# A two-layer Strassen kernel: the last visits' y sums are added on VectorE to loaded totals, and the second layer opens on such totals

## The chip, the core and the metric

One NeuronCore of a Trainium2 chip runs the whole program. The metric is device time in microseconds (us) of one execution; lower is better. Engines are named as the profile names them: PE (TensorE), DVE (VectorE), ACT (ScalarE), POOL (GpSimd) and SP (SyncE, which here only issues DMAs).

## The reference

Decayed causal attention gives 2304 tokens of width 512, and two feed-forward layers (512 to 2048 and back) follow. All is float32.

```python
scores = scale * np.matmul(q, k.transpose(0, 1, 3, 2))
ret = scores * Dmat                       # gamma ** (i - j) for i >= j, else 0
x = np.matmul(ret, v)                     # 4 x 8 heads, 576 x 64, laid out as 2304 x 512
h = x @ w_in                              # layer one
g = h * np.tanh(np.log1p(np.exp(np.minimum(h, 20.0))))   # h > 20 uses h inside tanh
x = g @ w_out
h = np.maximum(x @ moe2_w_in, 0.0)        # layer two
out = h * h @ moe2_w_out
```

## The kernel before, in words

**Visits.** The two layers m = 0, 1 are cut into 4 passes p over the 2048 hidden units, and each pass visits the three token blocks v of 768 tokens. That makes 24 visits u, 0 to 11 in layer one and 12 to 23 in layer two. The order of the blocks turns round from pass to pass, so that visits 9 to 11 have the blocks 2, 1, 0, visits 12 to 14 again 2, 1, 0, visits 18 to 20 have 2, 1, 0 and visits 21 to 23 have 0, 1, 2: visits 20 and 21 share block 0.

**Products.** A visit has two halves (fp 0, 1), each a Strassen-Winograd scheme of seven products P1 to P7 (`chain`, line 849 issues the matmuls). A product reads one of seven x operands, the tiles `ring` (ring_71 to ring_77), each held as a high and a low part, so that three matmuls make one product of float32 accuracy. The results pile up in four PSUM banks `h`, with copies of some of them in `cp`. ACT applies mish or relu, DVE or ACT squares, and differences and cuts into high and low parts (L750, L757) make operands `g` for the way back.

**y sums.** From the fourth visit of a layer on, the way back to width 512 is also seven products, R1, R2, R6, R5, R7, R4, R3 (`block_y`, L1002), into four PSUM banks `py`. The sums of visit u are made during visit u + 1, woven between its products; those of visit 23 come at the end. Each R belongs to one of four blocks of y (`R_TO`: R1 and R2 to 0, R4 to 1, R6 and R3 to 2, R5 and R7 to 3). A sum leaves PSUM by an ACT copy into a staging tile (`staging`: st_more, two tiles e, and t2, t3), where R2 is added on DVE to what R1 left (L1011); then POOL issues an accumulating DMA that adds the staging tile into DRAM: into the scratch `sums_d` (xsum_103 to 114, L1021) in layer one, into the output itself in layer two (L1023), whose runs there are 1 KB long. Six accumulates leave per visit.

**The last visit.** `load_total` (L1033) loads the four blocks of token block 2's sums from `out` into `total` (in part_69) at the start of visit 23; visit 23's own sums are added to them on DVE and stored plainly.

**The turn.** Visit 12 needs x operands of layer two for block 2, which is also visit 9's and whose sums are accumulated during visit 10. `again_x` loads blocks of xsum (seven loads, into the low halves of ring tiles and into t2), makes the four differences on DVE (L408, L409, L410, L417) and cuts each operand (`cut_x`: ACT makes the high part, DVE at L291 the low part). In the other visits `fetch` loads ready operands that were saved to DRAM (`ring<-d`).

**The order.** Every instruction goes into a `Plan` with its engine, a cost and the names (keys) that it reads and writes. `due` gives each a due time, working back from the order of the matmuls; `order` then simulates the engines and puts instructions in the order in which it would start them, the earliest due first among those that are ready. Matmuls stay nearly in the written order (`sequences`); DVE, ACT and SP are free to move. SP issues plain DMAs in that one order, and POOL's queue has the accumulates. `hand_over` passes a region of memory from one set of keys to another, here the half of part_69 that holds weights (`wy`) and then `total`.

```python
        if end:
            to, kt = (lambda: total[b]), [("total", b, i) for i in range(2)]
        else:
            to, kt = held.pop(b) if merged else staging(u)
        ...
            if merged or end:
                fn = lambda dst=dst, src=src: nc.vector.tensor_tensor(dst(), src(), dst(), op=ALU.add)
                dve(fn, n, [("py", o), kt[i]], [kt[i]])
            else:
                act(dst, src, n=n, reads=[("py", o)], writes=[kt[i]])
```

Of the kernel before, what the change touches and what calls it, by code (L numbers as in the profile page):

```python
# [19 lines left out]
DM = H * D  # L20
# [209 lines left out]
def kernel(  # L230
# [58 lines left out]
    def pair(op, out, a, b, n, reads, writes):  # L289
        get = lambda t: t() if callable(t) else t  # L290
        dve(lambda: nc.vector.tensor_tensor(get(out), a, get(b).bitcast(F32), op=op), n, reads, writes)  # L291

# [401 lines left out]
    def staging(u):  # L694
        slots = stage if fast(u) else first_stage
        if fast(u) and (u >= turn_m or 2 * NSB <= u < turn_m - 2):
            slots = slots + [(t.rearrange("p j n -> p (j n)"), [k, k]) for t, k in ((t2, "t2"), (t3, "t3"))]
        if u >= nv - 2:
            slots = slots[1:]
# [218 lines left out]
    def sum_keys(m, v, b):  # L918
        return [("sum", m, v, b, i) for i in range(3)]

    def out_block(v, b):
        r = SB * v + b // 2 * TH
        return out[r : r + TH, b % 2 * 256 : b % 2 * 256 + 256].rearrange("(i p) c -> p i c", p=P)

    def y_group(u, th, f):
# [27 lines left out]
        for i, o in enumerate(yb[0]):  # L953
            y = lambda o=o, n=TH if m == 0 else DM: py[o][:, :n]
            if m:
                t, kt = staging(u)
                r = SB * v + TH * th + P * i
                act(t()[:, :DM], y, n=DM, reads=[("py", o)], writes=kt)
                dma(out[r : r + P], t()[:, :DM], kt, [("sum", m, v, 2 * th + d, i) for d in range(2)], P * 4 * DM)
                continue  # L960
# [10 lines left out]
    def block_y(u, name):  # L971
# [4 lines left out]
        b = R_TO[name]  # L976
        end = u == nv - 1
        merged = name in MERGED and not end
        if end:
            to, kt = (lambda: total[b]), [("total", b, i) for i in range(2)]  # L980
        else:
            to, kt = held.pop(b) if merged else staging(u)
            if name == "R1" and "R2" in MERGED:
                held[b] = to, kt
        parts = (TH, TH) if m == 0 else (DM, DM // 2)
        for i, o in enumerate(two):
# [22 lines left out]
            src = lambda o=o, n=n: py[o][:, :n]  # L1009
            if merged or end:  # L1010
                fn = lambda dst=dst, src=src: nc.vector.tensor_tensor(dst(), src(), dst(), op=ALU.add)  # L1011
                dve(fn, n, [("py", o), kt[i]], [kt[i]])
            else:
                act(dst, src, n=n, reads=[("py", o)], writes=[kt[i]])
            if end and name in ("R2", "R7", "R4", "R3"):
                k = ((0, 2), (2, 3))[i]
                src = total[b][:, 256 * k[0] : 256 * k[1]].rearrange("p (i c) -> p i c", c=256)
                dma(out_block(v, b)[:, k[0] : k[1]], src, [kt[i]], [("out", b, i)], P * 4 * n)
        if not end and b not in held:
            if m == 0:  # L1020
                fn = lambda: nc.gpsimd.dma_start(out=sums_d[v][b], in_=in_two(to()), accum_op=ALU.add)  # L1021
            else:
                fn = lambda: nc.gpsimd.dma_start(  # L1023
                    out=out_block(v, b), in_=to().rearrange("p (i c) -> p i c", c=256), accum_op=ALU.add
                )
            plan.add("SP", 0.1, fn, kt, sum_keys(m, v, b), 2.6)
        late_cut = dict(R6=6, R5=2) if u == turn_m - 1 else dict(R1=6, R2=2)
        if name in late_cut or u != turn_m - 1:
# [3 lines left out]

    def load_total():  # L1033
        hand_over(ks_at[1], [("total", b, i) for b in range(4) for i in range(2)])
        v = visits[-1][2]
        for b in (0, 2, 3, 1):
            dst = total[b].rearrange("p (i c) -> p i c", c=256)
            dma(dst, out_block(v, b), sum_keys(1, v, b), [("total", b, i) for i in range(2)], P * 8 * TH)

# [47 lines left out]
    for u in range(nv + 1):  # L1087
# [15 lines left out]
        if u == turn_m + NSB:  # L1103
            free_ops[:] = [ahead[j] for j in (2, 4, 3, 1, 0)]
            free_raws.sort(key=lambda j: (j + 4) % 8)
            assert len(free_raws) == 8
        if u == nv - 1:
            load_total()
        pos = u % NSB
        for fp, seq in enumerate(sequences(u)):  # L1110
            if u in (NSB, turn_m + NSB):
                for name in ("R5", "R7", "R4", "R3") if fp else ("R1", "R2", "R6"):
                    split_block(name, visits[u][0])
            if (u, fp) == (1, 1):
                hand_over(part_keys(1), ks_at[1])
# [6 lines left out]
            for name in seq:  # L1122
# [121 lines left out]
```

## Time and profile before

| what | value |
|---|---|
| three timed runs | 803.25, 804.91, 805.34 us, median 804.91 |
| the profiled execution | 805.24 us, of which the span in the trace is 803.5 |
| mean granted clock of PE | 0.992 |
| busy: PE, PEld | 98%, 96% |
| busy: DVE, ACT, POOL | 82%, 70%, 15% |
| DMA | 212.07 MB, mean 264 GB/s |
| accumulates from staging, L1021 and L1023 | issued by POOL, 384 KB each |

The trace is of one execution. Busy shares are of its span; PE is the matmul pipe and PEld the weight loads beside it. The granted clock is a share of full speed. The time outside the span, 805.24 - 803.5 = 1.7 us, is start and end.

### The profile page before, as it was taken

To read this page: it belongs to the slowest core of one execution; us is meant where nothing else is said; L and a number is where in the kernel's file an instruction comes from. 1 tells how busy PE (TensorE), PEld (TensorE's weight loads), DVE (VectorE), ACT (ScalarE), POOL (GpSimd) and SP (SyncE) were. 2 spreads that over 40 slices of the span, in tenths; PEclk is the share of its full clock that TensorE was granted. 3 is DMA by queue.
4 is the path that set the end of the run, shared out by engine and by line. 5 is a ranking of instruction groups with operands and counts; after the bars stand their busy time and mean duration, and the time that the engine had idled before them with its cause. 6 is when DMAs were issued, how large, how long until landed. Compare 5 with 4: busy or idle time off the path is not lost.

```text
span 803.5 us, 14615 instructions
## 1 busy us (share of the span) xinstructions
PE 786.3 (98%) x5582; PEld 769.7 (96%) x5582; DVE 655.1 (82%) x1114; ACT 560.2 (70%) x1119; POOL 119.7 (15%) x122
## 2 busy tenths in 40 slices
PE   8999999999999999999989999999999999999797
PEld 7999999999999999998989898999999999999797
DVE  5799998887999875994768768989889977975537
ACT  1697667675887676875767677877788777885552
POOL 3200000001122111111110100001221231321220
PEclk9999999999999999999998999999999999999999
DMA  9984887369998997799999999669988999699975
GB/s 330 405 334 158 321 299 311 116 257 339 326 235 205 325 327 161 146 328 286 261 294 278 306 328 401 237 215 338 330 173 172 339 293 235 108 295 216 278 130 123
DMA packets 72966, 212.07 MB, mean 264 GB/s; under 512 B 6592, under 2 KB 29760, under 8 KB 72896
## 3 DMA queue, kind: packets, MB, share of 16 engines
q1 hardware_dynamic: 45920, 171.02, 56.6%
q0 software_dynamic: 26976, 40.11, 31.1%
q8 instruction: 44, 0.72, 0.4%
q14 instruction: 26, 0.21, 0.1%
HBM read 125.39 MB, written 85.72 MB: 263 GB/s over the span
## 4 chain that ended last, share of the span: by engine, by line
PE 85%; DVE 6%; DMA 6%; ACT 1%; issue 1%; SPq 1%; DVEq 0%; POOLq 0%; ACTq 0%
PE h L849 39%; PE py L1002 30%; PE py L944 12%; DMA ring<-d 2%; PE h L535 2%; PE py L589 1%; DMA out_dram<-t 1%; DMA out_dram<-e 1%; DVE ring L291 1%; DVE a L543 1%; PE py L553 1%; PE py L567 1%; DMA qk<-in_qk_dram 1%; DMA xraw<-part 1%; DVE g L750 1%
## 5 line engine op out<-in xcount | busy, mean ns | idle before, releaser
L849 PE MATMUL h<-ring,win 128*128 128x384 f32 x1932 | 369.3, 337 | 9.0 <-ACT cp L280 4.2
L849 PEld LDWEIGHTS h<-ring,win 128*128 128x128 f32 x1932 | 337.1, 189 | 11.6 <-ACT cp L280 4.4
L750 DVE TENSOR_TENSOR g<-part,g 128x768 fp32r<-128x768 f32 x126 | 119.3, 955 | 47.3 <-ACT g L280 47.0
L1002 PE MATMUL py<-wout,g 128*128 128x256 f32 x1134 | 147.7, 282 | 0.7 <-DVE g L750 0.7
L1002 PEld LDWEIGHTS py<-wout,g 128*128 128x128 f32 x1134 | 144.9, 190 | 0.9 <-DVE g L750 0.9
L1002 PE MATMUL py<-g,wout 128*128 128x384 f32 x756 | 144.5, 335 | 0.0
L1002 PEld LDWEIGHTS py<-g,wout 128*128 128x128 f32 x756 | 133.1, 189 | 0.0
L280 ACT ACTIVATE g<-part 128x768 fp32r<-128x768 f32 x126 | 105.0, 843 | 13.2 <-DVE part L757 8.4
L280 ACT ACTIVATE cp<-h 128x384 f32<-128x384 f32 x138 | 67.5, 489 | 38.9 <-PE h L849 37.9
L280 ACT ACTIVATE part<-h 128x384 f32<-128x384 f32 x108 | 52.7, 488 | 26.2 <-DVE h L832 19.7
L757 DVE TENSOR_TENSOR part<-part 128x768 f32<-128x768 f32 x72 | 66.6, 956 | 4.4 <-ACT part L280 3.0
L280 ACT ACTIVATE part<-py 128x384 f32<-128x384 f32 (+1 forms) x98 | 47.4, 509 | 30.2 <-PE py L944 17.0
L832 DVE TENSOR_TENSOR h<-h,cp 128x384 f32<-128x384 f32 x92 | 51.8, 564 | 16.6 <-PE h L849 16.5
L280 ACT ACTIVATE e<-py 128x384 f32<-128x384 f32 (+1 forms) x88 | 41.4, 489 | 23.8 <-PE py L1002 23.2
L1021 POOL DMA_DIRECT2D xsum<-part x19 | 16.9, 941 | 261.5 <-DVE part L1011 203.0
L1023 POOL DMA_DIRECT2D out_dram<-t x21 | 27.7, 1383 | 178.0 <-DVE t L1011 120.7
L944 PE MATMUL py<-g,wout 128*128 128x384 f32 x288 | 53.5, 335 | 0.4 <-DVE wout L291 0.4
L280 ACT ACTIVATE t<-py 128x512 f32<-128x512 f32 (+2 forms) x60 | 29.1, 489 | 33.5 <-PE py L1002 25.4
L944 PE MATMUL py<-wout,g 128*128 128x512 f32 x216 | 51.2, 391 | 0.0
L944 PEld LDWEIGHTS py<-g,wout 128*128 128x128 f32 x288 | 50.2, 188 | 0.7 <-DVE wout L291 0.7
L944 PEld LDWEIGHTS py<-wout,g 128*128 128x128 f32 x216 | 40.4, 188 | 8.0
L1021 POOL DMA_DIRECT2D xsum<-e x26 | 22.6, 880 | 92.3 <-ACT e L280 72.2
(95 smaller groups left out, 981.7 us busy)
## 6 DMA issues: line engine op xcount, KB each, us to landing
ring<-d SPq DMA_DIRECT2D x77, 768.0 KB, 8.6
raw<-in_wp_dram SPq DMA_DIRECT2D x64, 512.0 KB, 6.3
d<-ring SPq DMA_DIRECT2D x42, 768.0 KB, 7.4
xsum<-e POOLq DMA_DIRECT2D x26, 384.0 KB, 7.7
qk<-in_qk_dram SPq DMA_DIRECT2D x16, 512.0 KB, 8.2
out_dram<-t POOLq DMA_DIRECT2D x21, 384.0 KB, 9.4
xsum<-part POOLq DMA_DIRECT2D x19, 384.0 KB, 7.6
ring<-xsum SPq DMA_DIRECT2D x18, 384.0 KB, 5.0
```

Source lines behind the costliest of these rows:

```text
L280: fn = lambda: nc.scalar.activation(out() if callable(out) else out, in_() if callable(in_) else in_, func, **kw)
L291: dve(lambda: nc.vector.tensor_tensor(get(out), a, get(b).bitcast(F32), op=op), n, reads, writes)
L535: nc.tensor.matmul(psc[2 * x0 + e][to, hp, :n], t[r, 1, hp], t[r, 0, hp], start=True, stop=True)
L543: dve(lambda a=a, ps=ps, m=m: nc.vector.tensor_tensor(a, ps, m, op=ALU.mult), NP * n, ["mask", "maskt", ks[e]], [("a", x0, e)])
L750: lambda: nc.vector.tensor_tensor(lo(), src, hi().bitcast(F32), op=ALU.subtract),
L757: dve(lambda: nc.vector.tensor_tensor(d, x, y, op=ALU.subtract), 768, kx + ky, kd)
L832: lambda: nc.vector.tensor_tensor(dst(), bank(b)(), late["cp"][j], op=ALU.add),
L849: nc.tensor.matmul(dst(), w[:, hw, wi, s], ring[i][:, hx, k], start=(new and k == 0 and n == 0), stop=(k == 1 and n == 2), skip_group_chec ...
L944: nc.tensor.matmul(y, st[:, a], mv[:, b], start=(f == 0 and k == 0), stop=(f == FPP - 1 and k == 2), skip_group_check=True,)
L1002: nc.tensor.matmul(dst, st, mv, start=first, stop=last, skip_group_check=True)
L1021: fn = lambda: nc.gpsimd.dma_start(out=sums_d[v][b], in_=in_two(to()), accum_op=ALU.add)
L1023: fn = lambda: nc.gpsimd.dma_start(out=out_block(v, b), in_=to().rearrange("p (i c) -> p i c", c=256), accum_op=ALU.add)
```

## The change

**Layer two's partial sums** go to new scratch tiles `sums_o` (osum_135 to 140, two per token block, 3 KB runs) and no more to `out`: both what the first visits store and what POOL accumulates.

**The last four visits** (u = 20 to 23) keep no staging: each R is added on DVE (L1026) to a total that `load_total` (L1066) has loaded. Visits 20 and 21, both of token block 0, share the totals in the four tiles [e0, t3, e1, t2] (`wide`), loaded at the start of visit 21; visit 22 uses the four tiles of `total`, visit 23 `wide` again. The sums of visits 21 to 23 are then complete and are stored plainly into `out` (L1033).

**The turn.** The sums of visit 9 (u = turn_m - 3) are added in the same way, in visit 10, to the four totals t2, e1, e0 and st_more; only R6 is copied by ACT, into e0, and the loaded total (t3) is added to it. They are not stored. `turn_x` (L1079, L1080, L1081, L1087) makes visit 12's x operands from these four tiles, with the same differences and cuts as `again_x` but no loads. Which staging tiles visits 8, 10 and 19 use is set by small tables.

```diff
@@ block_y
-        end = u == nv - 1
+        end = u >= nv - 4 or u == turn_m - 3
         merged = name in MERGED and not end
         if end:
-            to, kt = (lambda: total[b]), [("total", b, i) for i in range(2)]
+            to, kt = totals_of(u)[b]
+        elif u == nv - 5 and not merged:
+            to, kt = last_stage[name]
+        elif u == turn_m - 4 and not merged:
...
+        elif u == turn_m - 2 and name == "R1":
+            to, kt = pairs[1]
+        elif u == turn_m - 2 and not merged:
...
-            if merged or end:
+            if merged or end and (m or name != "R6"):
                 fn = lambda dst=dst, src=src: nc.vector.tensor_tensor(dst(), src(), dst(), op=ALU.add)
                 dve(fn, n, [("py", o), kt[i]], [kt[i]])
             else:
                 act(dst, src, n=n, reads=[("py", o)], writes=[kt[i]])
-            if end and name in ("R2", "R7", "R4", "R3"):
...
+            if u > nv - 4 and name in ("R2", "R7", "R4", "R3") and (i or u == nv - 1):
+                k = ((0, 2), (2, 3))[i] if u == nv - 1 else (0, 3)
...
         if not end and b not in held:
...
+            fn = lambda: nc.gpsimd.dma_start(
+                out=sum_block(m, v, b), in_=to().rearrange("p (j n) -> p j n", **cut), accum_op=ALU.add
+            )
             plan.add("SP", 0.1, fn, kt, sum_keys(m, v, b), 2.6)
+        if u == turn_m - 3 and name == "R6":
+            dve(lambda: nc.vector.tensor_tensor(to(), to(), pairs[1][0](), op=ALU.add), 768, [*kt, "t3"], kt)
@@ new beside it
+    sums_o = [[dram_p.tile([2, P, 3, 2 * P], F32, tag=f"osum{v}_{t}", name="osum") for t in range(2)] for v in range(NSB)]
+    def sum_block(m, v, b):
+        return sums_o[v][b // 2][b % 2] if m else sums_d[v][b]
+    wide = [stage[1], pairs[1], stage[2], pairs[0]]
+    turn_total = [pairs[0], stage[2], stage[1], spare]
+    def totals_of(u):
+        return turn_total if u == turn_m - 3 else part_total if u == nv - 2 else wide
+    def load_total(u):
+        m, _, v = visits[u]
         for b in (0, 2, 3, 1):
+            to, kt = totals_of(u)[b] if m or b != 2 else pairs[1]
+            cut = dict(j=3 if m else 2)
+            fn = lambda to=to, b=b: nc.sync.dma_start(out=to().rearrange("p (j n) -> p j n", **cut), in_=sum_block(m, v, b))
+            plan.add("SP", 0.45, fn, sum_keys(m, v, b), kt, P * 3072 / 0.40e6)
+    def turn_x(name):
...
+        if name in ("P1", "P2", "P3"):
+            j = i if i < 2 else 3
+            cut_x(i, two(j), *kb[j])
+        elif name == "P5":
+            dve(lambda: tt(t3, two(3)(), two(2)(), op=ALU.subtract), 768, [*kb[3], *kb[2]], ["t3"])
+            dve(lambda: tt(t1, two(2)(), t2, op=ALU.subtract), 768, [*kb[2], "t2"], k1)
+            dve(lambda: tt(t2, two(3)(), t1, op=ALU.subtract), 768, [*kb[3], *k1], ["t2"])
...
@@ the loop over visits
-        if u == nv - 1:
-            load_total()
+        if u == turn_m - 2:
+            load_total(u - 1)
+        if u in (nv - 3, nv - 1):
+            load_total(nv - 4 if u == nv - 3 else nv - 1)
...
+            if (u, fp) == (nv - 2, 1):
+                hand_over(ks_at[1], [("total", b, i) for b in range(4) for i in range(2)])
+                load_total(nv - 2)
...
+                            elif u + 1 == turn_m:
+                                turn_x(name)
```

**What moves, on DVE at the turn.** Before, from the last addition into a bank of visit 11 (h_90) to visit 12's second product (h_92<-h_92,cp_1112) and on. sums_88, t2_97 and t3_98 hold differences of x blocks, L291 makes the low parts of the operands ring_71 to ring_77.

```order
L832 TENSOR_TENSOR h_90<-h_90,cp_1110 128x384
L291 TENSOR_TENSOR ring_71<-ring_71 128x768
L291 TENSOR_TENSOR ring_72<-ring_72 128x768
...
L832 TENSOR_TENSOR h_92<-h_92,cp_1112 128x384
...
L409 TENSOR_TENSOR sums_88<-ring_74,t2_97 128x768
L408 TENSOR_TENSOR t3_98<-ring_75,ring_74 128x768
L410 TENSOR_TENSOR t2_97<-ring_75,sums_88 128x768
L291 TENSOR_TENSOR ring_74<-sums_88,ring_74 128x768
L291 TENSOR_TENSOR ring_76<-t3_98,ring_76 128x768
L291 TENSOR_TENSOR ring_75<-t2_97,ring_75 128x768
```

After, the same stretch (e_1120, e_1121 and part_69 are totals; h_90<-h_90,cp_1116 is the last addition of visit 11, h_92<-h_92,cp_1118 visit 12's second product):

```order
L1080 TENSOR_TENSOR sums_88<-e_1120,t2_97 128x768
...
L1081 TENSOR_TENSOR t2_97<-part_69,sums_88 128x768
L291 TENSOR_TENSOR ring_72<-e_1121,ring_72 128x768
...
L291 TENSOR_TENSOR ring_74<-sums_88,ring_74 128x768
L291 TENSOR_TENSOR ring_75<-t2_97,ring_75 128x768
...
L291 TENSOR_TENSOR ring_77<-t2_97,ring_77 128x768
L830 TENSOR_TENSOR h_90<-h_90,cp_1116 128x384
...
L291 TENSOR_TENSOR ring_73<-part_69,ring_73 128x768
...
L830 TENSOR_TENSOR h_92<-h_92,cp_1118 128x384
```

Five of the seven cuts stood behind visit 12's second product with the differences; now all seven stand ahead of it, and six of them, with the differences, ahead of visit 11's last addition.

**What moves, on SP's queue in visits 10 and 11.** Before, the x operands of visit 11 (ring<-d_149 to d_155) follow each other, with weights (raw) ahead of them:

```order
L294 DMA ring_73<-d_137 128x1536
L294 DMA raw_80<-in_wp2_dram 128x1024
L294 DMA raw_81<-in_wp2_dram 128x1024
L294 DMA ring_71<-d_149 128x1536
L294 DMA ring_72<-d_150 128x1536
L294 DMA ring_75<-d_153 128x1536
```

After (the numbers of the d tiles are shifted by six):

```order
L294 DMA ring_73<-d_143 128x1536
L1066 DMA part_69<-xsum_114 128x768
L294 DMA raw_80<-in_wp2_dram 128x1024
L294 DMA raw_81<-in_wp2_dram 128x1024
L294 DMA ring_71<-d_155 128x1536
L1066 DMA e_1121<-xsum_112 128x768
L1066 DMA t3_98<-xsum_113 128x768
L294 DMA ring_72<-d_156 128x1536
L294 DMA ring_75<-d_159 128x1536
```

Three loads of totals have come in; a fourth (t2_97<-xsum_111) stands ahead of the x operands of visit 10.

**What moves, on SP's queue in visit 22.** Before, the seven x operands of visit 23 (ring<-d_156 to d_162) follow each other, and the totals of visit 23 come behind them:

```order
L294 DMA ring_77<-d_162 128x1536
L294 DMA ring_73<-d_158 128x1536
L294 DMA part_69<-out_0_dram 128x3x256 x4
L294 DMA out_0_dram<-part_69 128x2x256
```

After, from the first store of a finished block on (osum_139 is token block 2's scratch, osum_137 and osum_138 are block 1's):

```order
L1033 DMA out_0_dram<-e_1120 128x3x256
L1066 DMA e_1120<-osum_139 128x768
L1066 DMA part_69<-osum_137 128x768
L1066 DMA part_69<-osum_138 128x768 x2
L294 DMA ring_71<-d_162 128x1536
L1066 DMA part_69<-osum_137 128x768
L294 DMA ring_72<-d_163 128x1536
L1033 DMA out_0_dram<-t2_97 128x3x256
L294 DMA ring_75<-d_166 128x1536
L294 DMA ring_74<-d_165 128x1536
L1033 DMA out_0_dram<-t3_98 128x3x256
```

Loads of totals and stores of finished blocks now stand between the x operands.

## Rows read from the trace of the kernel before

**Rows 1.** The page's first part: busy time of each engine.

```profile
PE 786.3 (98%) x5582; PEld 769.7 (96%) x5582; DVE 655.1 (82%) x1114; ACT 560.2 (70%) x1119; POOL 119.7 (15%) x122
```

**Rows 2.** Windows of 5 us; columns in the first line.

```profile
core 0: us, PE busy (x) PEld busy (x) DVE busy (x) ACT busy (x) POOL busy (x), PEclk, DMA share, GB/s
360.00:365.00 5.00, 4.15 (x23) 3.54 (x21) 3.92 (x8) 2.00 (x4) 0.00 (x0) 1.00 1.05 303
365.00:370.00 5.00, 4.22 (x23) 3.96 (x24) 1.51 (x2) 2.10 (x4) 0.69 (x1) 1.00 0.73 257
...
415.00:420.00 5.00, 4.34 (x26) 4.02 (x24) 5.00 (x8) 4.26 (x7) 0.16 (x1) 1.00 1.06 324
420.00:425.00 5.00, 2.48 (x8) 2.48 (x9) 5.00 (x7) 3.76 (x8) 0.00 (x0) 0.65 0.85 288
...
755.00:760.00 5.00, 1.25 (x6) 1.25 (x7) 1.65 (x3) 3.29 (x6) 0.00 (x0) 0.94 1.19 221
760.00:765.00 5.00, 5.00 (x29) 5.00 (x28) 3.31 (x5) 2.94 (x7) 1.26 (x1) 0.72 0.48 139
```

**Rows 3.** Timeline, 720 to 804: start, us, engine, line, operation [idle before <-releaser].

```profile
756.71 0.87 ACT L280 ACTIVATE t<-py 128x512 f32<-128x512 f32 x2 [6.87 <-DMA out_dram<-t]
...
758.75 3.67 PE L849 MATMUL h<-ring,win 128*128 128x384 f32 x12 [4.22 <-ACT cp L280]
```

**Rows 4.** Chain of waits, 700 to 804: start, us, what.

```profile
734.32 10.69 DMA out_dram<-e
...
745.84 10.79 DMA out_dram<-t
...
758.75 3.67 PE h L849 x12
762.42 2.39 PE py L1002 x18
...
774.30 2.08 PE h L849 x12
776.39 2.15 PE py L1002 x18
```

**Rows 5.** Chain of waits, 340 to 445.

```profile
420.34 0.88 DVE sums L409
...
421.99 0.48 ACT e L280
...
422.52 4.21 PE h L849 x12
426.73 1.83 PE py L1002 x6
```

**Rows 6.** Timeline of PE, 778 to 804.

```profile
788.95 10.94 PE L1002 MATMUL py<-wout,g 128*128 128x256 f32 x89 [0.72 <-DVE g L750]
```

**Rows 7.** The page's third part: DMA queues, packets, MB, share of 16 engines.

```profile
q1 hardware_dynamic: 45920, 171.02, 56.6%
q0 software_dynamic: 26976, 40.11, 31.1%
```

**Rows 8.** Groups by form on DVE, 640 to 804 and 324 to 424: busy, mean ns.

```profile
L1011 DVE TENSOR_TENSOR part<-py,part 128x512 f32<-128x512 f32 x8 | 5.5, 690 | 2.0 <-PE py L1002 2.0
...
L1011 DVE TENSOR_TENSOR part<-py,part 128x256 f32<-128x256 f32 x8 | 3.4, 421 | 0.1
...
L1011 DVE TENSOR_TENSOR part<-py,part 128x384 f32<-128x384 f32 x2 | 1.1, 552 | 0.0
```

**Rows 9.** Windows of visits 10 and 21, columns as in rows 2.

```profile
353.30:384.85 31.55, 29.92 (x170) 29.05 (x169) 21.02 (x34) 18.61 (x37) 4.32 (x5) 1.00 0.97 294
690.90:720.50 29.60, 29.60 (x212) 29.60 (x211) 24.94 (x40) 24.11 (x50) 7.63 (x6) 1.00 0.77 198
```

**Rows 10.** Waits of SP's queue, 720 to 804: us in total, times, longest us.

```profile
SPq L294 <- DMA out_dram<-part: 12.3, 1, 12.3
```

**Rows 11.** Timeline, 700 to 705.

```profile
702.15 0.55 DVE L832 TENSOR_TENSOR part<-h,cp 128x384 f32<-128x384 f32 x1
...
703.60 1.73 PE L849 MATMUL h<-ring,win 128*128 128x384 f32 x9
```

More of the change, by code (lines that the diff above doesn't have):

```diff
@@ L956, in y_group @@
                 t, kt = staging(u)
-                r = SB * v + TH * th + P * i
                 act(t()[:, :DM], y, n=DM, reads=[("py", o)], writes=kt)
-                dma(out[r : r + P], t()[:, :DM], kt, [("sum", m, v, 2 * th + d, i) for d in range(2)], P * 4 * DM)
+                dst, src = sums_o[v][th][:, :, i].rearrange("d p c -> p d c"), t()[:, :DM].rearrange("p (d c) -> p d c", d=2)
+                dma(dst, src, kt, [("sum", m, v, 2 * th + d, i) for d in range(2)], P * 4 * DM)
                 continue
@@ L976, in block_y @@
         b = R_TO[name]
-        end = u == nv - 1
+        end = u >= nv - 4 or u == turn_m - 3
         merged = name in MERGED and not end
         if end:
-            to, kt = (lambda: total[b]), [("total", b, i) for i in range(2)]
+            to, kt = totals_of(u)[b]
+        elif u == nv - 5 and not merged:
+            to, kt = last_stage[name]
+        elif u == turn_m - 4 and not merged:
+            j = free_raws[0]
+            if name == "R3":
+                free_raws.append(free_raws.pop(0))
+            to, kt = turn_stage[name] if name != "R3" else ((lambda j=j: raw_g[j]), raw_keys[j])
+        elif u == turn_m - 2 and name == "R1":
+            to, kt = pairs[1]
+        elif u == turn_m - 2 and not merged:
+            free_raws.append(free_raws.pop(0))
+            to, kt = (lambda j=free_raws[-1]: raw_g[j]), raw_keys[free_raws[-1]]
         else:
             to, kt = held.pop(b) if merged else staging(u)
-            if name == "R1" and "R2" in MERGED:
-                held[b] = to, kt
+        if not end and name == "R1" and "R2" in MERGED:
+            held[b] = to, kt
         parts = (TH, TH) if m == 0 else (DM, DM // 2)
@@ L1014, in block_y @@
                 act(dst, src, n=n, reads=[("py", o)], writes=[kt[i]])
-            if end and name in ("R2", "R7", "R4", "R3"):
-                k = ((0, 2), (2, 3))[i]
-                src = total[b][:, 256 * k[0] : 256 * k[1]].rearrange("p (i c) -> p i c", c=256)
-                dma(out_block(v, b)[:, k[0] : k[1]], src, [kt[i]], [("out", b, i)], P * 4 * n)
-        if not end and b not in held:
[L1020 to L1025, printed above, removed]
+            if u > nv - 4 and name in ("R2", "R7", "R4", "R3") and (i or u == nv - 1):
+                k = ((0, 2), (2, 3))[i] if u == nv - 1 else (0, 3)
+                dst, src = out_block(v, b)[:, k[0] : k[1]], lambda k=k: to()[:, 256 * k[0] : 256 * k[1]]
+                fn = lambda dst=dst, src=src: nc.sync.dma_start(out=dst, in_=src().rearrange("p (i c) -> p i c", c=256))
+                plan.add("SP", 0.45, fn, kt[i:] if u == nv - 1 else kt, [("out", v, b, i)], P * 1024 * (k[1] - k[0]) / 0.40e6)
+        if not end and b not in held:
+            cut = dict(j=2) if m == 0 else dict(j=3)
+            fn = lambda: nc.gpsimd.dma_start(
+                out=sum_block(m, v, b), in_=to().rearrange("p (j n) -> p j n", **cut), accum_op=ALU.add
+            )
             plan.add("SP", 0.1, fn, kt, sum_keys(m, v, b), 2.6)
+        if u == turn_m - 3 and name == "R6":
+            dve(lambda: nc.vector.tensor_tensor(to(), to(), pairs[1][0](), op=ALU.add), 768, [*kt, "t3"], kt)
         late_cut = dict(R6=6, R5=2) if u == turn_m - 1 else dict(R1=6, R2=2)
@@ L1031, in block_y @@
             cut_op(u, late_cut[name])
-    def load_total():
-        hand_over(ks_at[1], [("total", b, i) for b in range(4) for i in range(2)])
-        v = visits[-1][2]
-        for b in (0, 2, 3, 1):
-            dst = total[b].rearrange("p (i c) -> p i c", c=256)
-            dma(dst, out_block(v, b), sum_keys(1, v, b), [("total", b, i) for i in range(2)], P * 8 * TH)
+    part_total = [((lambda b=b: total[b]), [("total", b, i) for i in range(2)]) for b in range(4)]
+    pairs = [((lambda t=t: t.rearrange("p j n -> p (j n)")), [k, k]) for t, k in ((t2, "t2"), (t3, "t3"))]
@@ new lines, in turn_x @@
+    def turn_x(name):
+        b, kb = zip(*turn_total)
+        two = lambda j: lambda: in_two(b[j]())
+        tt, i = nc.vector.tensor_tensor, X_AT[name]
+        t1 = sums.rearrange("p a n -> p (a n)").rearrange("p (k n) -> p k n", k=2)
+        k1 = [("s", j) for j in range(3)]
+        if name in ("P1", "P2", "P3"):
[5 more added lines that the diff above has]
+            dve(lambda: tt(t2, two(3)(), t1, op=ALU.subtract), 768, [*kb[3], *k1], ["t2"])
+            cut_x(4, t2, "t2")
+            cut_x(3, t1, *k1)
+        elif name == "P7":
+            cut_x(5, t3, "t3")
+        elif name == "P4":
+            dve(lambda: tt(t2, two(1)(), t2, op=ALU.subtract), 768, [*kb[1], "t2"], ["t2"])
+            cut_x(6, t2, "t2")
```

7 lines of the change are left out of this document (4 added, 3 removed).

## The prediction, made before the changed kernel ran

> **What bounds the kernel now.** I began with the page's first part: TensorE (PE) is busy for 786.3 of 803.5 us [rows 1]. Whatever the change does on other engines, it can win only what PE loses, so the question is where PE stands still and why. The busy time by stretches of 5 us finds the places: PE is short of 5.00 us at 360 to 370 (0.85 + 0.78 us), at 415 to 425 and at 755 to 760 (and, told below, at 789); the rows for 420 to 425 and for 760 to 765 show a second loss, a granted clock of 0.65 and 0.72, so that part of these stretches ran at the lower of the two levels (1.2 instead of 2.4 GHz) [rows 2]. The first two lie in the visits that end layer one, 415 to 425 is the turn into layer two, and 755 to 790 is the last visit and its sums.
>
> **Stall C, 754 to 764.** The timeline has PE idle for 4.22 us before visit 23's matmuls at 758.75, because ScalarE (ACT) had not copied its bank; ACT in turn stood 6.87 us before the copy of y into a staging tile, until an accumulate into out had read that tile [rows 3]. The chain of waits goes on from there: the accumulate took 10.79 us, and it was issued only when the one before it, into the same block, had landed after 10.69 us [rows 4]. After the idle time 12 products took 3.67 us where 12 take 2.08 at full clock, and 18 matmuls of the sums 2.39 where 18 take 2.15 [rows 4]: 1.59 + 0.24. Stall C costs 4.22 + 1.83 = 6.05 us.
>
> **Stall B, 419 to 429, the turn.** PE is idle 0.66 us of 415 to 420 and 2.52 of 420 to 425 [rows 2], 3.18 us in all, until ACT has read a bank (e<-h) at 421.99 [rows 5]. The chain of waits goes back from there to DVE's difference at L409, made from freshly loaded blocks [rows 5]. Then 12 products of the same shape take 4.21 instead of 2.08 [rows 5, 4], and 6 matmuls of the sums, which are as wide, 1.83 instead of half of 2.08 [rows 5]: 2.13 + 0.79. Stall B costs 3.18 + 2.92 = 6.10 us.
>
> **Two small ones.** A: 0.85 + 0.78 = 1.63 us at 360 to 370 [rows 2], where x tiles of visit 10 land late. D: 0.72 us at 788.95, for a cut of g on DVE [rows 6]. All four are 14.50 us.
>
> **The change, part by part.**
> The tail. The sums of visits 20 to 22 no longer go through staging tiles and accumulates: 18 accumulates (6 per visit) leave, and with them both kinds of wait that make stall C, ACT's for a staging tile and POOL's for the earlier accumulate into the block. In their place stand 4 + 4 loads of totals, beside the 4 that stay for visit 23, and 8 stores. An accumulate's share of the 16 DMA engines: 31.1% of 803.5 us for 40.11 MB is 6.23 us per MB, 2.45 us for one of 0.393 MB; a plain transfer, 56.6% for 171.02 MB, is 2.66 us per MB, 1.05 us each [rows 7]. So 18 x 2.45 = 44 us of DMA work leave and 16 x 1.05 = 17 come: the tail's traffic falls. I take all of C: **-6.05**. Bounds: 0, if a new wait stops PE for as long in the same place, and -6.05.
>
> The sums on DVE. Six sums per visit change from an ACT copy to a DVE add of 0.690 + 0.421 = 1.11 us [rows 8]: 6.66 us more on DVE in each of visits 21, 22 and 23. In visit 10 the sums of visit 9 add 10 instructions of 0.552 [rows 8] and one of 768 columns, which I price at two of these, 1.10: 6.62 us. They lie beside PE as long as DVE has room. In visit 10 it has: 21.02 busy of 31.55 [rows 9]. In visit 21 it has 29.60 - 24.94 = 4.66 us, less than 6.66 [rows 9]; but in the changed order eight instructions of this stretch (six of the weights' conversion, two squares) stand earlier or on ACT, at no less than 0.42 each [rows 8], the shortest add's time, 3.4 us: some 28.2 of 29.6 us would be used. Cost taken: 0; without that cover it is the price of rival 3.
>
> The turn. The seven loads of x blocks go, and the cuts and differences read the totals where DVE left them. The order shows the differences of L1079 to L1081 ahead of most cuts and of the last products' sums, and every cut before the row (h_92<-h_92) that belongs to visit 12's second product; before, five of the seven stood behind that row. What stays is DVE's work itself, the same four differences and seven cuts, so I do not take all of B: I leave a wait as long as the only one on DVE that PE shows elsewhere, 0.72 us [rows 6], and take 6.10 - 0.72 = **-5.4**. Bounds: 0, DVE being as late as before, and -6.10.
>
> Stall A. One load of a total (t2) now stands ahead of visit 10's x tiles on SP: 1.05 us of DMA work in a stretch whose DMA engines are full (share 1.05 and then 0.73) [rows 2]. The accumulate of visit 9's first sums, which ran there, is gone: 2.45 us less. Between +1.05 and -1.63 I take **0**, since the load stands before the x tiles and the accumulate came after most of them.
>
> Stall D. Near the end DVE gets R3's and R4's adds of visit 22 in front of the cuts that D waits for, and PE gets half of R5 between R2 and R6 to fill the time. I take **0**, within 0.7 either way.
>
> Wider rows. Layer two's partial sums now lie in scratch tiles with 3 KB runs instead of 1 KB in out. No PE wait between 430 and 750 hangs on them: 0.
>
> The sum: 805.24 (the profiled run) - 6.05 - 5.4 = **793.8 us**. That run is 0.33 above the median of the three shown (804.91); I leave this difference in the range.
>
> **A wait in SP's queue.** SP issues in order, and the trace has it held for 12.3 us behind one load of a total that waited for an accumulate [rows 10]. The changed order puts three such loads (L1066) among the x tiles of visits 10 and 11, each behind an accumulate of visit 8, and in the tail stores (L1033), each behind an add, among the x tiles of visit 23. I price this at 0 in the sum, because those accumulates are issued a whole visit before the x tile that stands behind them may be overwritten, and the adds before the stores come with the sums of visit 21, while x tiles are wanted in visit 23. The Trainium skill, DMA: Bandwidth & Descriptors, section "Anatomy of one DMA", says that DMA engines don't wait on semaphores: the wait is spent on the issuing sequencer, before dispatch. By this rule whatever stands behind a total's load waits with it, and the sum would rise by the hold; the 12.3 us of the trace agree with it.
>
> **Rivals.**
> 1. The turn's stall stays, since DVE's work there is the same and visit 10 hands it more. For: DVE is 5.00 of 5.00 us busy from 415 to 420 and from 420 to 425 [rows 2]. Against: the differences now need no load. 805.24 - 6.05 = 799.2 us. Chance 0.17.
> 2. SP is held at a total's load in visit 10 and the x tiles of visit 11 land late, by as much as the trace has seen, 12.3 us: 793.8 + 12.3 = 806.1, no change that can be told. Against: see above. Chance 0.08.
> 3. Slower: DVE becomes the bound in visits 10 and 21. The last product of each half adds into a bank that DVE must have read first: that read begins at 702.15 and takes 0.55, the product starts at 703.60 [rows 11], so DVE may be 0.90 us later than now, and from there on each us is PE's. If nothing of the new adds were hidden there, 6.62 + 6.66 us, and each stop cost 1.83 of lower clock as in C, the time is 793.8 + 13.3 + 3.7 = 810.8 us. For: 31.6 of 29.6 us by the bare sum in visit 21. Against: the planner moved work out. Chance 0.05.
> That the change doesn't do what it says has no chance of its own: the accumulates are missing from the changed order.
>
> **How the numbers follow.** The forecast (both stalls gone, up to 1 or 2 us of new waits) gets 0.70. Its own range is 790.3 (all 14.50 us gone, less the 0.33 of the median) to 796. The range given reaches to rival 1 and so leaves out rivals 2 and 3: 790.3 to 799.5. This kernel's runs can tell 0.3%, 2.4 us, from nothing. Faster: 0.70 + 0.17 = 0.87; same: 0.08; slower: 0.05.
>
> **What would show it.** In the profile after: no PE wait of over 1 us at visit 23 and no granted clock under 1.00 after 430; the opening products of visit 12 back to back at 2.08 us for 12; DVE's busy time up by 3 x 6.66 + 6.62 = 26.6 us at most; no accumulate after those of visit 19's sums. Wrong would be: a PE wait for DVE (L1026 adds ahead of a product's sum) in visits 10 or 21, a PE wait for ring<-d in visit 11, or a stop at the turn that ACT or DVE ends as before.

## The result, and the profile after

The changed kernel takes **792.21 us** (median of four runs, 791.97 to 793.06) where the kernel before takes 804.08 (four runs, 803.18 to 805.34): a ratio of **0.9853**, 95% interval 0.9835 to 0.9872. The forecast was 793.8, between 790.3 and 799.5. The profiled execution took 793.06, with a span of 790.9.

The page's first part, after. PE is busy 5.0 us less than in [rows 1] (matmuls at the lower clock count as busy for longer), while the span is 12.6 us shorter: the other 7.6 were standing still.

```profile
PE 781.3 (99%) x5582; PEld 765.5 (97%) x5582; DVE 673.0 (85%) x1154; ACT 547.6 (69%) x1080; POOL 79.8 (10%) x98
```

The windows of the changed kernel at the places of [rows 2], with the same columns. Stalls A, B and C are gone, the clock is at 1.00 in all of them; the last two rows show PE short of 5.00 us near the end, which ended at 787.4.

```profile
360.00:365.00 5.00, 4.99 (x29) 4.70 (x28) 5.00 (x11) 2.77 (x5) 0.00 (x0) 1.00 1.04 342
...
420.00:425.00 5.00, 5.00 (x31) 5.00 (x30) 5.00 (x11) 4.34 (x12) 0.62 (x1) 1.00 0.89 341
...
755.00:760.00 5.00, 5.00 (x36) 5.00 (x36) 4.20 (x7) 2.65 (x6) 0.00 (x0) 1.00 0.00 0
...
770.00:775.00 5.00, 4.42 (x37) 4.22 (x36) 4.99 (x8) 2.95 (x5) 0.00 (x0) 1.00 0.22 76
785.00:790.00 5.00, 1.33 (x9) 0.92 (x8) 1.78 (x4) 0.00 (x0) 0.00 (x0) 1.00 0.54 179
```

To see what each part is worth, compare stages that hold the same matmuls. Windows of the kernel before: visit 12 up to visit 13's first product, the first half of visit 23, and from there to the last matmul (visit 10 is in [rows 9]).

```profile
413.97:463.57 49.60, 46.42 (x229) 43.22 (x229) 40.26 (x63) 34.87 (x67) 6.07 (x7) 0.93 0.99 297
750.14:769.91 19.77, 15.55 (x98) 15.35 (x97) 8.51 (x12) 9.47 (x19) 2.56 (x2) 0.91 0.97 221
769.91:799.90 29.99, 29.26 (x223) 28.85 (x222) 19.92 (x31) 12.64 (x23) 5.11 (x4) 1.00 0.55 100
```

The changed kernel: visit 10, visit 11, visit 12, visit 21, the first half of visit 23, and the end.

```profile
353.56:382.93 29.37, 29.36 (x169) 29.07 (x169) 26.46 (x47) 15.32 (x27) 0.07 (x1) 1.00 0.95 347
382.93:412.05 29.12, 29.12 (x169) 29.12 (x169) 29.12 (x44) 25.51 (x47) 5.18 (x6) 1.00 0.88 249
412.05:455.52 43.47, 43.47 (x230) 40.58 (x229) 38.35 (x63) 33.86 (x64) 5.31 (x6) 1.00 1.02 316
682.72:712.30 29.58, 29.58 (x212) 29.58 (x211) 27.28 (x45) 20.43 (x38) 0.00 (x0) 1.00 0.60 195
741.96:755.70 13.74, 13.74 (x98) 13.74 (x97) 10.73 (x17) 8.18 (x14) 0.00 (x0) 1.00 0.67 261
755.70:787.45 31.75, 29.75 (x223) 28.96 (x222) 22.14 (x35) 11.36 (x19) 0.00 (x0) 1.00 0.22 72
```

| stage | forecast | measured |
|---|---|---|
| A, visit 10 (31.55 to 29.37) | 0 | **-2.2** |
| B, visit 12 (49.60 to 43.47) | -5.4 | -6.1 |
| C, visit 23's first half (19.77 to 13.74) | -6.05 | -6.0 |
| D, the end (29.99 to 31.75) | 0 | **+1.8** |

The sum, -12.5, is the gap between the last matmuls (799.90 and 787.45). Two terms that I had set at nothing were off in opposite directions. The new waits at the end, in the timeline of PE after:

```profile
774.48 3.86 PE L1017 MATMUL py<-wout,g 128*128 128x256 f32 x30 [0.57 <-DVE e L1026]
778.64 6.71 PE L1017 MATMUL py<-wout,g 128*128 128x256 f32 x54 [0.31 <-DVE e L1026]
786.46 0.98 PE L1017 MATMUL py<-wout,g 128*128 128x256 f32 x6 [1.11 <-DVE t L1026]
```

### The profile page after: what moved, and what is told of

Same layout as the page of the kernel before. It is cut to its first block, busy times and chain, and to the rows that moved or that the text cites. A ratio compares the mean times of both kernels' runs of the same rounds, so it can differ in the third digit from the quotient of the medians.

```text
span 790.9 us, 14588 instructions
## 1 busy us (share of the span) xinstructions
PE 781.3 (99%) x5582; PEld 765.5 (97%) x5582; DVE 673.0 (85%) x1154; ACT 547.6 (69%) x1080; POOL 79.8 (10%) x98
## 4 chain that ended last, share of the span: by engine, by line
PE 94%; DVE 4%; DMA 1%; issue 0%; SPq 0%; ACT 0%; ACTq 0%; DVEq 0%
PE h L847 42%; PE py L1017 33%; PE py L947 12%; PE h L535 2%; PE py L589 2%; PE py L553 1%; PE py L567 1%; DMA qk<-in_qk_dram 1%; PE h L901 1%; DVE ring L291 0%; DVE g L298 0%; DVE g L748 0%; DVE y L336 0%; DVE e L1026 0%; DVE a L543 0%
## 5 line engine op out<-in xcount | busy, mean ns | idle before, releaser
L847 PE MATMUL h<-ring,win 128*128 128x384 f32 x1932 | 365.1, 335 | 0.0
L1037 POOL DMA_DIRECT2D xsum<-part x22 | 19.3, 878 | 253.7 <-DVE part L1026 192.5
L280 ACT ACTIVATE e<-py 128x384 f32<-128x384 f32 (+1 forms) x64 | 30.0, 487 | 17.4 <-PE py L1017 17.2
L280 ACT ACTIVATE wout<-part 128x512 fp32r<-128x512 f32 x40 | 25.0, 629 | 7.6 <-PE py L1017 3.5
L280 ACT ACTIVATE t<-py 128x384 f32<-128x384 f32 (+2 forms) x38 | 18.4, 487 | 14.4 <-PE py L1017 13.8
L280 ACT ACTIVATE part<-part 128x384 f32<-128x384 f32 x36 | 18.9, 526 | 13.5 <-DVE part L830 13.1
```

The costliest lines, as they stand in the source:

```text
L280: fn = lambda: nc.scalar.activation(out() if callable(out) else out, in_() if callable(in_) else in_, func, **kw)
L847: nc.tensor.matmul(dst(), w[:, hw, wi, s], ring[i][:, hx, k], start=(new and k == 0 and n == 0), stop=(k == 1 and n == 2), skip_group_chec ...
L1037: fn = lambda: nc.gpsimd.dma_start(out=sum_block(m, v, b), in_=to().rearrange("p (j n) -> p j n", **cut), accum_op=ALU.add)
```

## The experiments

Theory at this point: each part of the change removes its own stall (the sums on DVE at the end C, the totals at the turn B and A), and the end got dearer by 1.8. Rivals: the wider rows of layer two's partial sums did it, the loads' place did it, or DVE is simply full at the end. The quoted texts are expectations, written before each run.

**One part at a time.** In the first kernel the turn is put back:

```diff
-        end = u >= nv - 4 or u == turn_m - 3
+        end = u >= nv - 4
...
-                            elif u + 1 == turn_m:
-                                turn_x(name)
```

> The last four visits as in the changed kernel, the turn as before. Theory (each part removes its own stall): visit 23 starts its products without the 4.22 us stop and takes 13.7 us to its second half instead of 19.8, the end costs 1.8 more than before as in the changed kernel, and visits 10 (31.5 us) and 12 (49.6 us to visit 13) stay as they were: 804.1 - 6.0 + 1.8 = 799.9 us. Rival (the parts lean on each other, as layer two's wider rows or freed tiles also help the turn): visit 12 or 10 gets shorter too and the time is under 797.

It took 799.3 us, ratio 0.995 (0.9930 to 0.9969) of a median of 803.16 for before. Visit 10 and visit 12 are as before, C is gone; PE waits 0.57, 0.30 and 1.11 us at the end.

```profile
353.68:384.92 31.24, 29.60 (x169) 29.02 (x169) 21.01 (x34) 18.56 (x37) 4.34 (x5) 1.00 1.00 301
414.04:463.51 49.47, 46.30 (x230) 43.09 (x229) 40.26 (x63) 34.85 (x67) 6.09 (x7) 0.93 0.99 300
750.07:763.81 13.74, 13.74 (x98) 13.74 (x97) 10.73 (x17) 8.17 (x14) 0.00 (x0) 1.00 0.70 265
```

In the second the last visits and the place of the partial sums are put back, though the line that plans the last visit's stores is the new one:

```diff
-        end = u >= nv - 4 or u == turn_m - 3
+        end = u == nv - 1 or u == turn_m - 3
...
-        return sums_o[v][b // 2][b % 2] if m else sums_d[v][b]
+        return out_block(v, b) if m else sums_d[v][b]
```

> The turn as in the changed kernel, the last visits and layer two's partial sums in the output as before. Theory: visit 10 29.4 us, visit 12 43.5 us to visit 13, the 4.22 us stop of visit 23 stays, and the end is as before: 804.1 - 2.1 - 6.1 = 795.9 us. Rival (the late x tiles of visit 10 went for another reason than the turn's part): visit 10 stays at 31.5 and the time is 798.

798.17 us, ratio 0.9938 (0.9907 to 0.9969). Visits 10 and 12 are those of the changed kernel, and C is there (3.62 us idle). Of the 2.3 us over the expectation 1.8 lie at the end, which takes 31.75 us here too, with the same three waits. So **the end's loss is not the price of visit 22's adds**, which are not in it.

```profile
355.39:384.56 29.17, 29.17 (x170) 29.14 (x170) 26.49 (x47) 15.33 (x27) 0.07 (x1) 1.00 0.94 345
413.68:457.14 43.46, 43.46 (x229) 40.57 (x229) 38.39 (x63) 33.75 (x64) 5.37 (x6) 1.00 1.03 320
743.59:762.75 19.16, 15.54 (x99) 15.22 (x97) 9.06 (x13) 8.67 (x18) 2.17 (x3) 0.91 0.93 227
762.75:794.50 31.75, 29.74 (x223) 28.96 (x222) 18.81 (x29) 13.77 (x25) 5.52 (x5) 1.00 0.56 97
```

```profile
781.52 3.86 PE L1017 MATMUL py<-wout,g 128*128 128x256 f32 x30 [0.57 <-DVE part L1026]
785.68 6.71 PE L1017 MATMUL py<-wout,g 128*128 128x256 f32 x54 [0.30 <-DVE part L1026]
793.51 0.98 PE L1017 MATMUL py<-wout,g 128*128 128x256 f32 x6 [1.11 <-DVE part L1026]
```

**What removed C.** The third kernel has nothing of the change but that store line and layer two's partial sums in scratch tiles, with 3 KB rows; the last visits and the turn are as before. Against the kernel before:

```diff
-                dma(out[r : r + P], t()[:, :DM], kt, [("sum", m, v, 2 * th + d, i) for d in range(2)], P * 4 * DM)
+                dst, src = sums_o[v][th][:, :, i].rearrange("d p c -> p d c"), t()[:, :DM].rearrange("p (d c) -> p d c", d=2)
+                dma(dst, src, kt, [("sum", m, v, 2 * th + d, i) for d in range(2)], P * 4 * DM)
...
+        return sums_o[v][b // 2][b % 2] if m else sums_d[v][b]
```

> The kernel before with nothing but layer two's partial sums in scratch tiles of 3 KB runs; sums of visits 20 to 22 still go by staging and accumulates. Left out: the finished blocks of token blocks 0 and 1 are not carried into the output. Theory (the stop at visit 23 comes from two accumulates into one block, one behind the other): the accumulates still wait for each other and the stop stays over 2 us: 802 to 804. Rival (it was the accumulates' 1 KB rows): an accumulate takes half of its 10.7 us, the stop goes, and the time is 798 with no sum moved to DVE.

799.03 us, ratio 0.9937 (0.9917 to 0.9958). The theory fell and the rival held: C is gone with every accumulate still there.

```profile
413.25:461.59 48.34, 45.17 (x230) 41.96 (x229) 40.26 (x63) 34.84 (x67) 6.07 (x7) 0.96 1.01 303
749.01:762.75 13.74, 13.74 (x99) 13.74 (x98) 8.41 (x12) 9.40 (x19) 1.72 (x2) 1.00 1.04 332
```

POOL's timeline shows how. First the kernel before, then with wide rows, in the same place of visit 22: the accumulate that has to land before the next into its block holds POOL 4.81 us instead of 10.25, and its issue takes 0.86 us instead of 1.26. Over the whole run they differ less: from issue to landing, the median of the accumulates of tiles t is 7.6 us against 9.4, that of e 6.7 against 9.3, that of part 7.8 against 8.3. The length of the rows and their place (scratch, not the output) changed together, and no run tells which of the two counts.

```profile
734.32 1.26 POOL L1023 DMA_DIRECT2D out_dram<-e  x1 [1.43 <-ACT e L280]
745.84 2.57 POOL L1023 DMA_DIRECT2D out_dram<-t  x2 [10.25 <-DMA out_dram<-e]
```

```profile
733.18 0.86 POOL L1027 DMA_DIRECT2D osum<-e  x1 [3.59 <-ACT e L280]
738.86 0.86 POOL L1027 DMA_DIRECT2D osum<-t  x1 [4.81 <-DMA osum<-e]
```

The counterpart keeps the sums on DVE and goes back to 1 KB rows in the output:

```diff
-        return sums_o[v][b // 2][b % 2] if m else sums_d[v][b]
+        return out_block(v, b) if m else sums_d[v][b]
...
+                dma(out[r : r + P], t()[:, :DM], kt, [("sum", m, v, 2 * th + d, i) for d in range(2)], P * 4 * DM)
```

> The changed kernel, but layer two's partial sums and totals lie in the output itself, in 1 KB runs, as before. Theory (the last visits' sums on DVE leave no accumulate at visit 23 to wait for, whatever the rows): visit 23's first half still takes 13.7 us and the time is 791.5 to 794. Rival (the stop went only with the wider rows): loads and accumulates in 1 KB rows stop PE again at visits 21 to 23 by over 2 us: 795 to 798.

One run, 792.3 us (before beside it 803.22), and visit 23's first half is as short. **Either part alone removes C**; together they save no more than one.

```profile
741.21:754.95 13.74, 13.74 (x99) 13.74 (x97) 10.72 (x17) 8.18 (x14) 0.00 (x0) 1.00 0.71 265
```

**What removed B.** Three kernels ask what made visit 12's operands late. In the first, visit 9's sums go by accumulates again (`end = u >= nv - 4`), and four totals are loaded in visit 11 into the four free tiles:

```diff
-        if u == turn_m - 2:
-            load_total(u - 1)
+        if u == turn_m - 1:
+            load_total(u - 2)
```

> The changed kernel, but visit 9's sums are staged and accumulated as before; in visit 11 the four totals are loaded from DRAM into the four free tiles, and visit 12's x operands are made from them. Theory (the turn's stop came from loads that had to wait for ring tiles of visit 11, so that DVE's differences began at 420 after DVE had stood idle): four loads into tiles outside the ring do as well as the adds: visit 12 to 13 within 1 us of 43.5, and 792 to 795 in all, more only if the late x tiles of visit 10 come back. Rival (only sums that never leave the chip are early enough): the stop at visit 12 stays at 3 us or more: 797 to 800.

794.62 us, ratio 0.9882 (0.9859 to 0.9904). B is gone without one of visit 9's adds on DVE; A has come back, as the expectation allowed.

```profile
353.56:385.05 31.49, 29.74 (x169) 29.00 (x169) 22.33 (x38) 18.89 (x36) 5.27 (x6) 1.00 1.00 300
414.17:457.90 43.73, 43.73 (x229) 40.56 (x229) 40.50 (x65) 31.49 (x63) 5.18 (x6) 1.00 1.02 299
```

In the second the adds stay, and the totals go to DRAM and come back into the ring tiles:

```diff
+        if u == turn_m - 3 and name in ("R2", "R7", "R4", "R3"):
+            dma(sums_d[v][b], in_two(to()), kt, sum_keys(m, v, b), P * 8 * TH) if not callable(to) else plan.add("SP", 0.45, lambda: nc.sync.dma_start(out=sums_d[v][b], in_=in_two(to())), kt, sum_keys(m, v, b), P * 8 * TH / 0.40e6)
...
-                            elif u + 1 == turn_m:
-                                turn_x(name)
```

> The changed kernel, but visit 9's totals, added on DVE, are stored to DRAM and visit 12's x blocks are loaded into the ring tiles and t2 as before, seven loads. Theory (loads into ring tiles can start only when visit 11 has used them, so the differences come after 413 and DVE's nine operations pile up): the stop at visit 12 comes back, 2.5 to 3.5 us idle and 49 us to visit 13 instead of 43.5: 796 to 799. Rival (what made the loads late was the accumulates before them): with early plain stores the stop stays away, under 1 us: 792 to 794.

One run, 794.24 us. It fell between the two: 1.11 us of idle, 44.86 us to visit 13. With the sums made early, loading the blocks into ring tiles costs 1.4 of the 6.1 us.

```profile
411.93:456.79 44.86, 43.75 (x229) 40.54 (x229) 41.88 (x66) 36.10 (x68) 5.25 (x6) 1.00 1.04 333
```

In the third nothing is moved or taken away; the kernel before is only told to count on the loads sooner:

```diff
-        dma(dst, src, ks, [kd], P * 8 * TH, early=early, slack=2.0)
+        dma(dst, src, ks, [kd], P * 8 * TH, early=early, slack=2.0 - trust[0])
...
+                                trust[0] = 5.0 if u + 1 == turn_m else 0.0
```

> The kernel before, with the plan told that visit 12's x blocks land 5 us sooner; no instruction is added or taken away, but on DVE the differences and the cuts now stand ahead of visit 12's second product. Theory (the blocks had landed at 413.8, and DVE's order kept the first difference until 420.25): it starts by 417, PE's 3.18 us at 419 shrink by half or more, visit 12 takes 44 to 47 us to visit 13 instead of 49.6, about 799 to 801. Rival (the loads themselves are too late): the differences wait on DVE for their loads, what stands behind them waits too, and visit 12 takes 49 us or more: 803 or over.

One run, 804.37 us beside a median of 803.89: the total did not move. By the profiles the turn gained 3.25 us and later stages lost most of them: 2.2 on the way to visit 23 (288.74 us against 286.57, with a new stop of 0.87 in visit 20) and 0.8 in visit 23's first half (20.60 against 19.77). The turn itself did as the theory said, apart from the idle time, which fell from 3.18 to 0.64 + 1.68 us, less than by half: the first difference starts at 415.05, right behind its load, and visit 12 takes 46.35 us.

```profile
413.36:459.71 46.35, 44.03 (x229) 40.51 (x229) 39.56 (x62) 35.58 (x67) 5.44 (x6) 1.00 1.01 303
```

```profile
415.05 0.96 DVE L411 TENSOR_TENSOR sums<-ring,t 128x768 f32<-128x768 f32 x1 [0.43 <-DMA ring<-xsum]
...
419.53 2.18 PE L851 MATMUL h<-ring,win 128*128 128x384 f32 x11 [0.64 <-DVE ring L291]
423.39 1.32 PE L851 MATMUL h<-ring,win 128*128 128x384 f32 x6 [1.68 <-ACT cp L280]
```

So a part of B was the plan's caution, which set the differences later on DVE than the data came: 3.25 of the 6.1 us against the kernel before. Only 0.86 of them are idle time. The other 2.39 are busy time (46.42 to 44.03 us), with the granted clock at 1.00 instead of 0.93, and that share varies: three more kernels with the same turn (wide rows, and the two below) take 48.34, 48.49 and 48.49 us, all with 3.17 or 3.18 us idle and a clock of 0.96. Against these the caution is worth 2.0 to 2.1 us. That the rest was data that came late fits the loads into free tiles, which have almost all of it, but is not shown by itself.

The five kernels line up. The difference into sums starts, counted from visit 12's start, at +6.3 us (before), +1.7 (this one), -1.2 (totals by DRAM), -4.5 (loads into free tiles) and -12.2 (the changed kernel, where another difference stands ahead of it, at 394.90); this goes with 49.6, 46.35, 44.86, 43.73 and 43.47 us. The rows are those of before, of totals by DRAM, of loads into free tiles and of the changed kernel:

```profile
420.25 0.96 DVE L409 TENSOR_TENSOR sums<-ring,t 128x768 f32<-128x768 f32 x1
410.73 0.95 DVE L409 TENSOR_TENSOR sums<-ring,t 128x768 f32<-128x768 f32 x1
409.69 0.95 DVE L1073 TENSOR_TENSOR sums<-e,t 128x768 f32<-128x768 f32 x1
399.83 0.95 DVE L1080 TENSOR_TENSOR sums<-e,t 128x768 f32<-128x768 f32 x1
```

**What removed A.** In the kernel before, PE waits between 350 and 372 for x tiles alone:

```profile
PE h L849 <- DMA ring<-d: 1.6, 3, 1.2
```

Two kernels leave accumulates out of the kernel before, and keep every other instruction in its place.

```diff
+            if u == 8 and name in ("R7", "R4", "R3"):
+                fn = lambda: None
```

> The kernel before, with three accumulates of visit 8's sums (R7, R4 and R3, issued at 347.05, 348.09 and 351.44, ahead of the last x tiles of visit 10) left out; every other instruction stays in place. Theory (visit 10's x tiles landed late because these stood in the same full DMA engines): three times 2.45 us of DMA work less, the last x tiles land some 5 us earlier, the 1.63 us of idle at 361 to 368 are gone and visit 10 takes 29.2 instead of 31.5: about 802. Rival (it was visit 9's first accumulate, issued at 358.66): visit 10 stays at 31.5.

```diff
+            if u == 9 and name == "R2":
+                fn = lambda: None
```

> The kernel before, with the first accumulate of visit 9's sums (R1 with R2, issued at 358.66) left out; all else in place. Theory (the accumulates before the last x tile decide): visit 10's x tiles land at most 1.5 us earlier, and over half of the 1.63 us of idle at 361 to 368 stays. Rival (this accumulate, which the change takes away too, is the cause): the idle is gone and visit 10 takes 29.2 us.

801.87 and 800.66 us, one run each beside 803.22. Single runs cannot tell times so close; the stage can: **each of them empties stall A**, and visit 10 takes 29.12 us in both. For the second the rival was right: one accumulate of 384 KB, issued 7 us after the last x tile's load, was enough to make these tiles late, with the three of visit 8 ahead of it. The last x tile took 16.6 us from issue to landing in the kernel before and 13.9 without it; without the other three it took 8.4.

```profile
353.51:382.63 29.12, 29.12 (x169) 29.12 (x169) 20.84 (x34) 18.51 (x37) 4.33 (x5) 1.00 0.84 264
```

```profile
352.81:381.93 29.12, 29.12 (x169) 29.12 (x169) 20.83 (x34) 18.50 (x37) 3.47 (x4) 1.00 0.95 302
```

**The loss at the end.** The changed kernel and the six above that have its store line take 31.7 us at the end; the kernels without that line take 30.0. It has the first store of a total read `kt[i:]`, both parts, so the plan sets the add of the second part behind this store's landing (the totals in t2 and t3 have one name for both parts besides); PE's order and DVE's follow. In DVE's timeline of the changed kernel the row at 785.39 holds two adds, R4's first part and, behind it, R7's second part. PE's last matmuls need the bank that the second one reads, and the first one waits for PE (1.46 us):

```profile
785.39 1.02 DVE L1026 TENSOR_TENSOR t<-py,t 128x512 f32<-128x512 f32 x2 [1.46 <-PE py L1017]
786.33 0.41 DVE L1026 TENSOR_TENSOR e<-py,e 128x256 f32<-128x256 f32 x1
787.48 0.42 DVE L1026 TENSOR_TENSOR t<-py,t 128x256 f32<-128x256 f32 x1 [0.74 <-PE py L1017]
```

```diff
-                plan.add("SP", 0.45, fn, kt[i:] if u == nv - 1 else kt, [("out", v, b, i)], P * 1024 * (k[1] - k[0]) / 0.40e6)
+                plan.add("SP", 0.45, fn, [kt[i]] if u == nv - 1 else kt, [("out", v, b, i)], P * 1024 * (k[1] - k[0]) / 0.40e6)
```

> The changed kernel with one word less: each store of the last visit reads only its own part (kt[i] for kt[i:]). Totals in t2 and t3 have one name for both parts, so their second add still stands behind the first part's store. Theory: the first two waits of the end (0.57 and 0.31 us) go, and the 1.11 us before the last sum, which is behind t2, stays: 791 to 791.6. Rival (DVE is full): all three stay.

One run, 791.39 us. As expected the 0.57 and 0.31 are gone, and the 1.11 behind t2 stays; what was not expected is that the 0.72 us of before [rows 6] are back. The end takes 31.34 us, so the word alone gives back 0.4 of the 1.8.

```profile
754.78:786.12 31.34, 29.50 (x223) 28.89 (x222) 22.16 (x35) 11.36 (x19) 0.00 (x0) 1.00 0.23 77
...
773.82 10.22 PE L1017 MATMUL py<-wout,g 128*128 128x256 f32 x83 [0.72 <-DVE g L748]
785.15 0.97 PE L1017 MATMUL py<-wout,g 128*128 128x256 f32 x6 [1.11 <-DVE t L1026]
```

The last kernel also plans both stores of a sum behind both adds, so that the one name of t2's two parts (and of t3's) does no harm:

```diff
+                stores.append((fn, [kt[i]] if u == nv - 1 else kt, i, P * 1024 * (k[1] - k[0]) / 0.40e6))
+        for fn, ks, i, size in stores:
+            plan.add("SP", 0.45, fn, ks, [("out", v, b, i)], size)
```

> The changed kernel, with the plan told of the last visit's stores only after both adds of a sum, and each store reading only its own part. Theory (the 0.57, 0.31 and 1.11 us at the end come from the changed store, which the plan lets read both parts of a total, so that it sets the second add behind the first part's store and orders PE and DVE by that): the waits at the end shrink to the 0.7 us of before or less, PE's last sums run in the order of before, and the time is 1.3 to 2 us under the changed kernel's: 790.2 to 791 where that has 792.2. Rival (DVE is simply full at the end, with visit 22's adds on it): the waits stay at 1.5 us or more and the time is the same.

> The changed kernel once more, as the measure for the run beside it on the same chip: 792 us, 0.985 of before.

**790.52 us** (789.99 to 791.3), ratio 0.9833 (0.9812 to 0.9854), against 792.88 (791.29 to 794.78), ratio 0.9859 (0.9834 to 0.9884), for the changed kernel on the same chip. The intervals overlap, so the total times alone don't tell the two apart; the stage does. The end takes 29.98 us, what it took before, with the one wait of before:

```profile
753.73:783.71 29.98, 29.26 (x223) 28.86 (x222) 22.13 (x35) 11.36 (x19) 0.00 (x0) 1.00 0.24 79
```

```profile
772.77 10.94 PE L1017 MATMUL py<-wout,g 128*128 128x256 f32 x89 [0.72 <-DVE g L748]
```

At the end this version is 1.8 us shorter than the changed kernel, with DVE as busy (22.13 against 22.14 us). DVE was not full at the end; it was told to wait.

## Why the prediction was right, and where it was not

**The frame held**: what could be won was PE's time of standing still and slow clock, 14.5 us by the prediction, and 12.5 came. The range held, too (its lower end is 790.4 by its own sum, not 790.3). That the forecast lies within 0.8 us of the profiled run is in part luck: A gave 2.2 us and D took 1.8, both set at nothing.

**C, -6.05**: measured -6.0, the size was right. Of the mechanism half was missing. I gave it all to the accumulates that leave and set the wider rows at 0, looking for waits between 430 and 750 only. The run with wide rows alone shows that they remove C, and the run with 1 KB rows and the sums on DVE that these do, too.

**B, -5.4**: measured -6.1. The remainder of 0.72 us that I kept for DVE was not there; the opening products of visit 12 run back to back. The cuts' place in DVE's order was a good part of it, and rival 1 (DVE's work keeps the stall) fell. What I had not separated is why they stood late: 2.0 to 3.3 us of B were the plan's allowance for a load, not the load. The size that I gave B, 6.10, is that of one execution; where the lower clock lasted less long the same turn lost 1.1 to 1.3 us less.

**A, 0**: measured -2.2, beyond the bound of -1.63. The step that failed is "the accumulate came after most of them". It came after all x tiles' issues, and delayed them all the same, since they were still under way in full DMA engines; the run without it measured it at the whole of A, as did the run without the three before it. The bound was too tight because I counted idle time alone: visit 10 takes 2.43 us more than the 29.12 that it takes without a stop, of which 1.63 are idle and 0.80 longer busy time (29.92 us). The extra load of a total, which I set against it, cost visit 10 at most 0.25 us (29.37 against 29.12), and nothing in the second profile of the changed kernel (29.12).

**D, 0 within 0.7**: measured +1.8, outside the bound. The step that failed is that it was read from what DVE has to do. I did not follow the store's reads through the plan, neither the one changed word nor the single name of t2's and t3's parts, though the order of PE's last sums had visibly changed. The sign that no PE wait at visit 23 would be over 1 us failed with it: one of 1.11 us stands in that visit's sums.

**DVE's room**: in visit 21 it is busy 27.28 us of 29.58, where I had 28.2; in visit 10 26.46 of 29.37, where the sum gives 21.02 + 6.62 = 27.6. Visit 11 is the tightest, 29.12 of 29.12, and PE still waits for nothing there: rival 3 did not come, but nothing is left. DVE's total rose by 17.9 us, below the 26.6 given as the most.

**The wait in SP's queue** (rival 2): visit 11 takes 29.12 us, with no wait of PE, so the price of 0 held. What the Trainium skill says of the issuing sequencer (DMA: Bandwidth & Descriptors, "Anatomy of one DMA") was not put to the test by a hold that mattered.

Left open: why runs of one kernel show stops in single visits now and then (1.15 us in visit 20 of the changed kernel's second profile).

## What to carry to other kernels

When a change has two parts that each shorten the same wait, price them together and test each alone: here wider rows would have done for C what moving 18 sums to DVE did. Where a planner orders the engines, read its dependences as closely as the instructions: one store that named a tile part too many was enough to cost 1.8 us where each part had a name of its own (the kernel with the turn alone), and where two tiles had one name for both parts, mending the word gave back only 0.4; one over-careful landing time cost 2 to 3 us of a 5 to 6 us stall. A DMA that is issued later than another made it late here, while both were under way.

## What was not expected of the hardware

A load of an x tile is in flight long enough in full DMA engines (share 1.05 in [rows 2]) that a single 384 KB accumulate, issued 7 us behind the last of them, costs PE 1.63 us of idle and visit 10 2.4 us; without it, or without the three accumulates ahead of it, nothing. Rows of 3 KB in scratch instead of 1 KB in the output changed POOL's time for issuing an accumulate from 1.26 to 0.86 us, and POOL's wait for one to land, in one place beside other transfers, from 10.25 to 4.81 us. And the same stop of 3.2 us at the turn was followed by more or less time at the lower clock from one profiled execution to the next: 12 products took 3.76 to 4.21 us behind it, where they take 2.08 at full clock.
